# Sliding-window attention in front of a gated feed-forward: from two stages to one woven schedule

## The chip, the cores and the metric

The kernel runs on one core of a Trainium2 chip. A core has five engines, each with an instruction queue of its own that it works through in order: TensorE (PE in the profile, with its weight loads shown as PEld), VectorE (DVE), ScalarE (ACT), GpSimd (POOL) and SyncE (SP). TensorE writes its results to PSUM, a small memory of eight banks, one of which holds a 128x512 fp32 tile; the other operands live in SBUF. DMA engines move data between main memory and SBUF; POOL and SP issue the transfers here. A DMA issued by POOL can convert fp32 to bf16 on its way, and all loads of this kernel do so.

The metric is the device time of one execution in microseconds (us). Lower is better.

## The reference

For 4 batches, 8 heads, 768 tokens and 64 channels a head, each token attends to the 128 latest tokens, itself included, and to the first 4 tokens of its batch (the sinks):

```python
keep = is_sink | in_window              # pos < 4, or 0 <= i - j < 128
scores = np.where(keep, scale * (q @ k.T), -1e9)
a = softmax(scores)
attn = a @ v                            # [4, 8, 768, 64]
```

The result, written as x with 3072 rows (batch, token) and 512 columns (head, channel), goes through a feed-forward with 1536 hidden channels:

```python
g = x @ w_gate
out = ((g * sigmoid(g)) * (x @ w_val)) @ w_out      # [3072, 512] fp32
```

## The kernel before

Two stages follow each other. In the attention stage a loop runs over 16 pairs of heads (4 batches, 2 heads at a time). `load_pair` loads q, k and v of a pair with six DMAs on POOL (lines 204 to 217; the first pair's k in four smaller ones). `prep_pair` transposes q and k in blocks of 128x128 on TensorE (line 231) and copies them from PSUM to SBUF on DVE (234). Then a loop runs over the 6 tiles of 128 tokens. `attn_scores` multiplies the tile's queries with up to three blocks of 128 keys: its own, the one before and the one that holds the sinks (line 254, keys on the output's partitions, 64 rows of the PE array a head), applies exp on ACT (261) and multiplies by a mask of zeros and ones on DVE (265). `attn_pv` multiplies by v, which carries a 65th column of ones so that the sum of each softmax row comes out beside the result (275), and DVE divides by that sum (282, 283). `flush_tile` transposes the normalised tile on TensorE (291), and ACT copies it into xT (292), which holds the whole transposed x.

The feed-forward stage, `ffn_chunks`, runs over 6 blocks of 512 tokens. For each of 12 slices of 128 hidden channels four matmuls of 512 columns give the gate, `pg` (line 138), four more the value, `pv` (144); ACT computes Silu (149) and DVE the product (150). Then 4 down tiles of 128 tokens take 12 matmuls each (157), ACT copies the result (162), and POOL and SP in turn issue the store (163).

The six PSUM pools have one buffer for each of their names, and several names are used in turn by both stages. The order of the program text isn't the order of the run: the framework's scheduler orders each engine's instructions by its own priorities and buffers. So the weights' 20 DMAs (lines 119 to 124), which the text places near the end of the attention stage, are issued well before it. A slot mechanism that would have let feed-forward pieces into the attention stage (`Feed`) is switched off.

## Time and profile before

| what | value |
|---|---|
| three timed runs, median (lowest to highest) | 376.04 us (375.91 to 376.06) |
| profiled execution: first to last instruction | 374.3 us |
| PE busy in it | 346.1 us (92%) |
| DVE, ACT, POOL busy | 154.9, 150.2, 104.2 us |
| read from, written to main memory | 28.31 MB, 6.29 MB |

The profile is of one execution, which has no separate time beside its span; the median lies 1.7 us above the span. PE's matmuls are pipelined and their ends are modelled: a matmul is shown as busy from its start until its result stands in PSUM, so short matmuls that wait for one another make PE look busy too. The groups of instructions give the busy time, then the mean duration of one in nanoseconds, then how long the engine had been idle before them and what ended that. The granted clock of TensorE is 0.999 of full speed over the span.

### The profile page before, as it was taken

How to read it: one execution, taken by the hardware profiler on the slowest of the kernel's cores; microseconds unless marked ns; L12 is line 12 of the kernel's file. 1: busy time of each engine (PE TensorE's matmuls, PEld its weight loads, DVE VectorE, ACT ScalarE, POOL GpSimd, SP SyncE). 2: the span in 40 equal slices, each digit the busy share in tenths (PEclk: the TensorE clock that was granted, in tenths of full speed). 3: DMA queues.
4: the chain of work that ended last, by engine and by line, in shares of the span. 5: the costliest groups of instructions: out<-in, count | busy, mean ns of one | idle time of the engine just before them, and what ended most of it. 6: DMA issues, size and time to landing. Idle time of an engine off the chain costs nothing.

```text
span 374.3 us, 5659 instructions
## 1 busy us (share of the span) xinstructions
PE 346.1 (92%) x2112; PEld 172.9 (46%) x2112; DVE 154.9 (41%) x440; ACT 150.2 (40%) x386; POOL 104.2 (28%) x155
## 2 busy tenths in 40 slices
PE   0689999999999999899999999999999999999995
PEld 0355555555555555554444444443444444444442
DVE  0466666666666666664330232033023203302320
ACT  1355555555655655566331332333133233313321
POOL 8997666965445551110001000000100000010000
PEclk9999999999999999999999999999999999999999
DMA  9999999998998983330001100200110020011002
GB/s 60 67 98 120 147 183 174 135 130 59 60 64 59 57 59 21 23 21 2 0 0 58 56 0 12 103 0 3 56 56 2 3 109 2 0 56 58 0 10 102
DMA packets 80890, 20.80 MB, mean 56 GB/s; under 512 B 76000, under 2 KB 77536, under 8 KB 80864
## 3 DMA queue, kind: packets, MB, share of 16 engines
q0 software_dynamic: 79136, 17.31, 49.6%
q1 hardware_dynamic: 1728, 3.15, 2.2%
q8 instruction: 16, 0.26, 0.3%
q14 instruction: 10, 0.08, 0.1%
HBM read 28.31 MB, written 6.29 MB: 92 GB/s over the span
## 4 chain that ended last, share of the span: by engine, by line
PE 85%; POOL 5%; ACT 4%; DMA 2%; issue 2%; DVE 0%; POOLq 0%; ACTq 0%; DVEq 0%
PE pv L144 19%; PE pg L138 17%; PE po L157 17%; PE ps L254 15%; PE po L275 8%; PE pt L231 7%; ACT pe L261 4%; PE px L291 3%; DMA wo<-in_moe_w_out_dram 1%; POOL va L217 1%; POOL qb L215 1%; DMA kb<-in_k_dram 1%; POOL kb L204 1%; POOL kb L211 0%; DVE ht L150 0%
## 5 line engine op out<-in xcount | busy, mean ns | idle before, releaser
L150 DVE TENSOR_TENSOR ht<-sg,pv 128x512 bf16<-128x512 bf16 x72 | 49.5, 687 | 135.5 <-PE pv L144 135.5
L261 ACT ACTIVATE pe<-ps 128x384 bf16<-128x384 f32 (+1 forms) x192 | 73.3, 435 | 79.2 <-PE po L275 64.6
L254 PE MATMUL ps<-qT,kT 64*128 64x128 bf16 x480 | 76.0, 293 | 9.4 <-ACT pe L261 6.9
L149 ACT ACTIVATE sg<-pg 128x512 bf16<-128x512 f32 x72 | 43.0, 597 | 83.5 <-PE pg L138 83.5
L138 PE MATMUL pg<-xT,wg 128*128 128x512 bf16 x288 | 75.4, 383 | 0.2 <-ACT pe L261 0.2
L144 PE MATMUL pv<-xT,wv 128*128 128x512 bf16 x288 | 74.8, 381 | 0.3 <-DVE ht L150 0.3
L157 PE MATMUL po<-wo,ht 128*128 128x512 bf16 x288 | 63.1, 379 | 0.0
L163 POOL DMA_DIRECT2D out_dram<-ot x12 | 6.6, 547 | 202.3 <-ACT ot L162 202.3
L254 PEld LDWEIGHTS <-kT 64*128 64x128 bf16 x480 | 34.4, 111 | 32.4 <-issue 15.4
L144 PEld LDWEIGHTS <-wv 128*128 128x128 bf16 x288 | 27.9, 97 | 44.0 <-issue 18.2
L275 PE MATMUL po<-va,pe 128*128 128x65 bf16 x480 | 44.5, 244 | 1.6 <-DVE an L283 1.5
L157 PEld LDWEIGHTS <-ht 128*128 128x128 bf16 x288 | 28.2, 98 | 34.0
L138 PEld LDWEIGHTS <-wg 128*128 128x128 bf16 x288 | 28.2, 98 | 33.8 <-issue 0.6
L265 DVE TENSOR_TENSOR pe<-pe,mask_g 128x768 bf16<-128x768 bf16 x64 | 35.7, 557 | 18.0 <-ACT pe L261 16.3
L275 PEld LDWEIGHTS <-pe 128*128 128x128 bf16 x480 | 31.9, 128 | 15.9 <-issue 9.4
L162 ACT COPY ot<-po 128x512 f32<-128x512 f32 x24 | 14.1, 586 | 54.3 <-PE po L157 54.3
L217 POOL DMA_DIRECT2D va<-in_v_dram x32 | 26.4, 831 | 30.0 <-PE po L275 29.5
L215 POOL DMA_DIRECT2D qb<-in_q_dram x32 | 26.5, 835 | 18.7 <-PE pt L231 18.5
L231 PE MATMUL pt<-ident_b,kb 128*128 128x128 bf16 x96 | 18.0, 296 | 11.9 <-POOL ident_b masks.py:199 8.7
L211 POOL DMA_DIRECT2D kb<-in_k_dram x30 | 24.8, 838 | 13.0 <-PE po L275 11.0
L283 DVE TENSOR_TENSOR an<-po,rcp 128x128 bf16<-128x128 f32 x96 | 27.5, 286 | 1.3
L291 PE MATMUL px<-ident_b,an 128*128 128x128 bf16 x96 | 27.9, 290 | 0.1
(33 smaller groups left out, 146.6 us busy)
## 6 DMA issues: line engine op xcount, KB each, us to landing
qb<-in_q_dram POOLq DMA_DIRECT2D x32, 96.0 KB, 3.4
va<-in_v_dram POOLq DMA_DIRECT2D x32, 96.0 KB, 3.7
out_dram<-ot POOLq DMA_DIRECT2D x12, 256.0 KB, 2.3
out_dram<-ot SPq DMA_DIRECT2D x12, 256.0 KB, 2.0
kb<-in_k_dram POOLq DMA_DIRECT2D x30, 96.0 KB, 3.5
wg<-in_moe_w_gate_dram POOLq DMA_DIRECT2D x4, 384.0 KB, 6.8
wv<-in_moe_w_val_dram POOLq DMA_DIRECT2D x4, 384.0 KB, 6.5
wo<-in_moe_w_out_dram POOLq DMA_DIRECT2D x12, 128.0 KB, 4.4
```

The source lines that it names most:

```text
L138: nc.tensor.matmul(pg, wg[:, c, f * P:(f + 1) * P], xT[:, c, tb0:tb0 + TB], start=(c == 0), stop=(c == DMC - 1),)
L144: nc.tensor.matmul(pv, wv[:, c, f * P:(f + 1) * P], xT[:, c, tb0:tb0 + TB], start=(c == 0), stop=(c == DMC - 1),)
L149: nc.scalar.activation(sg, pg, AF.Silu)
L150: nc.vector.tensor_tensor(ht[:, f], sg, pv, op=ALU.mult)
L157: nc.tensor.matmul(po, ht[:, f, ts * P:(ts + 1) * P], wo[:, f], start=(f == 0), stop=(f == DFC - 1),)
L215: nc.gpsimd.dma_start(qb[:, :, hh], q[b, h + hh].rearrange(rr, p=P))
L231: nc.tensor.transpose(pt[:, j * P:(j + 1) * P], src[:, half * 3 + j], ident_b,)
L254: nc.tensor.matmul(pss[hh][:, j * P:(j + 1) * P], kT[r0:r0 + D, kv * P:(kv + 1) * P], qT[r0:r0 + D, t * P:(t + 1) * P], start=True, stop=True,
L261: nc.scalar.activation(pe[:, hh, :nb * P], pss[hh][:, :nb * P], AF.Exp, scale=scale)
L265: nc.vector.tensor_tensor(pe4, pe4, masks[t][:, :, :nb, :], op=ALU.mult,)
L275: nc.tensor.matmul(po[:, hh], pe[:, hh, j * P:(j + 1) * P], va[:, kv, hh], start=(j == 0), stop=(j == nb - 1),)
L291: nc.tensor.transpose(px, anat_tiles[t], ident_b)
```

## The change

The whole body of the kernel is replaced. The result is the same function.

- The order is fixed: under `manual_schedule` each engine gets its instructions in the order of the program text.
- Attention is cut into 12 groups of 256 tokens with all 8 heads. A group g belongs to batch b = g // 3 and stands at place c = g % 3 in it; c = 0 has no earlier keys. It consists of steps: T transposes q and k of a pair of heads (four times a group), S computes scores and exp of a pair (four times), K the sinks (once, if c > 0), PV multiplies 128 tokens and four heads by v (four times) and X transposes the result (twice). Masks, divisions and copies of X on DVE are put into a list, `later`, and issued at the end of the current piece.
- The sinks' scores for all heads come from four accumulating matmuls: `kss` holds the 4 sink keys of the 8 heads at 32 columns of their own, and `vsbs` the 4 sink values of each head in rows of their own. `step_ks` fills both, the second from `vcs`, which 8 small DMAs a batch bring.
- Groups 0 and 1 come first. In feed-forward block tb = 0 to 4 the steps of groups 2 tb + 2 and 2 tb + 3 are placed in 15 of 16 slots: a gate slot takes them between pg and pv, a down slot in the middle of its 12 matmuls.
- Silu becomes a tanh: (tanh(g/2) + 1) * g is twice Silu(g), and the final copy is scaled by 0.5. The tanh is kept in fp32.
- pg, pv and the down tiles share three PSUM buffers; scores have one (two banks), P·V results two, and one buffer serves T, K and X. xT holds two blocks.
- The loads of groups 0 to 3 and of all weights, masks and small DMAs stand in one fixed order on POOL; the load of group g + 4 follows T of group g. All stores are issued by SP.

```diff
-            nc.scalar.activation(sg, pg, AF.Silu)
-            nc.vector.tensor_tensor(ht[:, f], sg, pv, op=ALU.mult)
-            yield
...
-            nc.scalar.copy(out=ot, in_=po)
-            (nc.sync if ts % 2 else nc.gpsimd).dma_start(
...
+    natp = pool("natp", 4)
+    vpool = pool("vpool", 1)
+    kqtp = pool("kqtp", 2)
+    epool = pool("epool", 3)
+    espool = pool("espool", 2)
+    xnp = pool("xnp", 3)
+    smallp = pool("smallp", 4)
+    xtp = pool("xtp", 2)
+    tpool = pool("tpool", 3)
+    upool = pool("upool", 3)
+    hpool = pool("hpool", 2)
+    opool = pool("opool", 4)
+    ps_f = pool("ps_f", 3, True)
+    ps_s = pool("ps_s", 1, True)
+    ps_o = pool("ps_o", 2, True)
+    ps_t = pool("ps_t", 1, True)
+    ctx.enter_context(tc.manual_schedule())
...
+    def load_group(g, split=1):
+        b, c = divmod(g, GC)
+        t0 = c * 256
+        kq = natp.tile([P, 2, 2, H * D], BF16, tag="kq", name="kq")
+        va = vpool.tile([P, 2, H, VS], BF16, tag=f"va{g}", name="va")
+        hn = H // split
+        for s in range(split):
+            hs = slice(s * hn, (s + 1) * hn)
+            for i, src in ((0, k), (1, q)):
+                for j in range(2):
+                    nc.gpsimd.dma_start(
+                        kq[:, i, j, s * hn * D:(s + 1) * hn * D].rearrange(
+                            "p (h d) -> p h d", d=D),
+                        src[b, hs, t0 + j * P:t0 + (j + 1) * P].rearrange(
+                            "h p d -> p h d"),
+                    )
+        for j in range(2):
+            nc.gpsimd.dma_start(
+                va[:, j, :, 0:D],
+                v[b, :, t0 + j * P:t0 + (j + 1) * P].rearrange("h p d -> p h d"),
+            )
+        nat[g], vas[g] = kq, va
...
+    def load_gate(i):
+        n = FG * P
+        for lst, w, nm in ((wgs, moe_w_gate, "wg"), (wvs, moe_w_val, "wv")):
+            t = wpool.tile([P, DMC, n], BF16, tag=f"{nm}{i}", name=nm)
+            nc.gpsimd.dma_start(
+                t, w[:, i * n:(i + 1) * n].rearrange("(c p) f -> p c f", p=P))
+            lst.append(t)
...
+    def load_out(i):
+        n = DFC // 4
+        t = wpool.tile([P, n, DM], BF16, tag=f"wo{i}", name="wo")
+        nc.gpsimd.dma_start(
+            t, moe_w_out[i * n * P:(i + 1) * n * P].rearrange("(c p) f -> p c f", p=P))
+        wos.append(t)
...
+    load_group(0, split=2)
+    make_identity(nc, ident)
...
+    load_group(1)
+    build_mask(mask0, True)
+    load_gate(0)
+    load_gate(1)
+    build_mask(mask, False)
+    load_gate(2)
+    load_gate(3)
+    load_group(2)
+    nc.gpsimd.memset(diag_h, 1.0)
+    nc.gpsimd.affine_select(
+        out=diag_h, in_=diag_h, compare_op=ALU.is_ge, fill=0.0, base=0,
+        pattern=[[-NS, H]], channel_multiplier=1)
+    nc.gpsimd.affine_select(
+        out=diag_h, in_=diag_h, compare_op=ALU.is_ge, fill=0.0, base=NS - 1,
+        pattern=[[NS, H]], channel_multiplier=-1)
+    KS = P + 2 * NS
+    for b in range(B):
+        vc = const.tile([P, D + 1], BF16, tag=f"vc{b}", name="vc")
+        nc.vector.memset(vc, 0.0)
+        nc.vector.memset(vc[:, D:D + 1], 1.0)
+        ks = const.tile([P, NP2 * KS], BF16, tag=f"ks{b}", name="ks")
+        nc.vector.memset(ks, 0.0)
+        vsb = const.tile([P, H, D + 1], BF16, tag=f"vsb{b}", name="vsb")
+        vcs.append(vc)
+        kss.append(ks)
+        vsbs.append(vsb)
+    for i in range(4):
+        load_out(i)
+    load_group(3)
+    for b in range(B):
+        for h in range(H):
+            nc.gpsimd.dma_start(vcs[b][h * NS:(h + 1) * NS, 0:D], v[b, h, 0:NS])
+    def ones_v(g):
+        nc.vector.memset(vas[g][:, :, :, D:D + 1], 1.0)
...
+    def flush():
+        for f in later:
+            f()
+        later.clear()
+    def step_T(g, p, on_dve=False):
+        b, c = divmod(g, GC)
+        if c == 0 and p == 0:
+            kqT[b] = kqtp.tile([P, NP2, 2, S], BF16, tag="kqT", name="kqT")
+        pt = ps_t.tile([P, 2, 2, P], BF16, tag="pt", name="pt")
+        for i in range(2):
+            for t in range(2):
+                nc.tensor.transpose(
+                    pt[:, i, t], nat[g][:, i, t, p * P:(p + 1) * P], ident)
+        dst = kqT[b][:, p, :, c * 256:(c + 1) * 256].rearrange(
+            "q i (t r) -> q i t r", t=2)
+        if on_dve:
+            nc.vector.tensor_copy(out=dst, in_=pt)
+        else:
+            nc.scalar.copy(out=dst, in_=pt)
+    def step_ks(g):
+        b = g // GC
+        dst = kss[b].rearrange("q (a m) -> q a m", m=KS)
+        for h in range(2):
+            r = slice(h * D, (h + 1) * D)
+            nc.vector.tensor_copy(
+                out=dst[r, :, h * NS:(h + 1) * NS], in_=kqT[b][r, :, 0, 0:NS])
+        nc.vector.tensor_tensor(
+            vsbs[b],
+            vcs[b].rearrange("q (o d) -> q o d", o=1).broadcast_to([P, H, D + 1]),
+            diag_h.rearrange("q (h o) -> q h o", o=1).broadcast_to([P, H, D + 1]),
+            op=ALU.mult)
+    def step_S(g, p):
+        b, c = divmod(g, GC)
+        if p == 0:
+            e_t[g] = epool.tile([P, H, 512], BF16, tag="e", name="e")
+        ps = ps_s.tile([P, 2, 512], FP32, tag="s", name="s")
+        kT, qT = kqT[b][:, p, 0], kqT[b][:, p, 1]
+        q0 = c * 256
+        parts = [(q0, q0, 256, P), (q0 + P, q0 + P, P, 3 * P)]
+        if c > 0:
+            parts.insert(0, (q0 - P, q0, P, 0))
+        for kk, qq, n, col in parts:
+            for h in range(2):
+                r = slice(h * D, (h + 1) * D)
+                nc.tensor.matmul(
+                    ps[:, h, col:col + n], kT[r, kk:kk + P], qT[r, qq:qq + n],
+                    start=True, stop=True)
+        lo = 0 if c > 0 else P
+        e = e_t[g][:, 2 * p:2 * p + 2, lo:512]
+        nc.scalar.activation(e, ps[:, :, lo:512], AF.Exp, scale=scale)
+        m = (mask if c > 0 else mask0).rearrange("q (o a) x -> q o (a x)", o=1)
+        def dve():
+            nc.vector.tensor_tensor(
+                e, e, m[:, :, lo:512].broadcast_to([P, 2, 512 - lo]), op=ALU.mult)
+        later.append(dve)
+    def step_K(g):
+        b, c = divmod(g, GC)
+        if c == 0:
+            return
+        ps = ps_t.tile([P, 256], FP32, tag="pt", name="pk")
+        for p in range(NP2):
+            nc.tensor.matmul(
+                ps, kss[b][:, p * P:(p + 1) * P],
+                kqT[b][:, p, 1, c * 256:(c + 1) * 256],
+                start=(p == 0), stop=(p == NP2 - 1))
+        es_t[g] = espool.tile([P, 256], BF16, tag="es", name="es")
+        nc.scalar.activation(es_t[g], ps, AF.Exp, scale=scale)
+    def step_PV(g, j, hh):
+        b, c = divmod(g, GC)
+        t = 2 * c + j
+        if hh == 0:
+            xns[g, j] = xnp.tile([P, DM], BF16, tag="xn", name="xn")
+        po = ps_o.tile([P, 4, D + 1], FP32, tag="o", name="o")
+        mms = []
+        if c > 0:
+            mms.append((po, es_t[g][:, j * P:(j + 1) * P],
+                        vsbs[b][:, 4 * hh:4 * hh + 4]))
+        for hq in range(4):
+            h = 4 * hh + hq
+            if t > 0:
+                vp = vas[g][:, 0, h, 0:D + 1] if j else vas[g - 1][:, 1, h, 0:D + 1]
+                mms.append((po[:, hq], e_t[g][:, h, 256 * j:256 * j + P], vp))
+            mms.append((po[:, hq], e_t[g][:, h, 256 * j + P:256 * (j + 1)],
+                        vas[g][:, j, h, 0:D + 1]))
+        for i, (o, l, r) in enumerate(mms):
+            nc.tensor.matmul(o, l, r, start=(i == 0), stop=(i == len(mms) - 1),
+                             skip_group_check=True)
+        def dve():
+            rcp = smallp.tile([P, 4, 1], FP32, tag="rcp", name="rcp")
+            nc.vector.reciprocal(rcp, po[:, :, D:D + 1])
+            nc.vector.tensor_tensor(
+                xns[g, j][:, 256 * hh:256 * (hh + 1)].rearrange(
+                    "p (h d) -> p h d", h=4),
+                po[:, :, 0:D], rcp.broadcast_to([P, 4, D]), op=ALU.mult)
+        later.append(dve)
+    def step_X(g, j):
+        tb, off = divmod(g * 256 + j * P, TB)
+        if off == 0:
+            xTs[tb] = xtp.tile([P, DMC, TB], BF16, tag="xT", name="xT")
+        pt = ps_t.tile([P, DMC, P], BF16, tag="pt", name="px")
+        for i in range(DMC):
+            nc.tensor.transpose(pt[:, i], xns[g, j][:, i * P:(i + 1) * P], ident)
+        def dve():
+            nc.vector.tensor_copy(out=xTs[tb][:, :, off:off + P], in_=pt)
+        later.append(dve)
+    def T(g, p):
+        def f(pro=False):
+            if p == 0:
+                ones_v(g)
+            step_T(g, p, on_dve=(pro and p % 2 == 1))
+            if p == NP2 - 1:
+                if g % GC == 0:
+                    later.append(lambda: step_ks(g))
+                if g + 4 < NG:
+                    load_group(g + 4)
+        return f
+    def A(fn, *a):
+        def f(pro=False):
+            if pro and fn is not step_S:
+                flush()
+            fn(*a)
+        return f
...
+    def gate(tb, f, attn):
+        fi, fo = divmod(f, FG)
+        fs = slice(fo * P, (fo + 1) * P)
+        if f == 0:
+            hts[tb] = hpool.tile([P, DFC, TB], BF16, tag="ht", name="ht")
+        x = xTs[tb]
+        pg = ps_f.tile([P, TB], FP32, tag="f", name="pg")
         for c in range(DMC):
+            nc.tensor.matmul(pg, wgs[fi][:, c, fs], x[:, c],
+                             start=(c == 0), stop=(c == DMC - 1))
+        th = tpool.tile([P, TB], FP32, tag="th", name="th")
+        nc.scalar.activation(th, pg, AF.Tanh, scale=0.5)
+        for a in attn:
+            a()
+        pv = ps_f.tile([P, TB], FP32, tag="f", name="pv")
+        for c in range(DMC):
+            nc.tensor.matmul(pv, wvs[fi][:, c, fs], x[:, c],
+                             start=(c == 0), stop=(c == DMC - 1))
+        u = upool.tile([P, TB], BF16, tag="u", name="u")
+        nc.vector.scalar_tensor_tensor(u, th, 1.0, pg, op0=ALU.add, op1=ALU.mult)
+        nc.vector.tensor_tensor(hts[tb][:, f], u, pv, op=ALU.mult)
+        flush()
+    def down(tb, ts, attn):
+        po = ps_f.tile([P, DM], FP32, tag="f", name="pd")
+        n = DFC // 4
         for f in range(DFC):
+            if f == DFC // 2:
+                for a in attn:
+                    a()
+            nc.tensor.matmul(
+                po, hts[tb][:, f, ts * P:(ts + 1) * P], wos[f // n][:, f % n],
+                start=(f == 0), stop=(f == DFC - 1))
+        ot = opool.tile([P, DM], FP32, tag="ot", name="ot")
+        nc.scalar.activation(ot, po, AF.Copy, scale=0.5)
+        nc.sync.dma_start(out[tb * TB + ts * P:tb * TB + (ts + 1) * P], ot)
+        flush()
+    def run(*steps):
+        for s in steps:
+            s(pro=True)
+            if len(later) > 1:
+                later.pop(0)()
+    def ts(g):
+        return [T(g, p) for p in range(NP2)], [A(step_S, g, p) for p in range(NP2)]
+    def px(g):
+        return ([A(step_PV, g, j, hh) for j in range(2) for hh in range(2)],
+                [A(step_X, g, j) for j in range(2)])
+    t0, s0 = ts(0)
+    t1, s1 = ts(1)
+    v0, x0 = px(0)
+    v1, x1 = px(1)
+    run(*t0)
+    run(s0[0], s0[1], s0[2], t1[0], s0[3], t1[1], t1[2], t1[3])
+    run(v0[0], s1[0], v0[1], s1[1], v0[2], s1[2], v0[3], s1[3],
+        A(step_K, 1), x0[0], x0[1])
+    run(*v1, *x1)
+    flush()
+    for tb in range(NTB):
+        slots = [[] for _ in range(16)]
+        if tb + 1 < NTB:
+            ga, gb = 2 * tb + 2, 2 * tb + 3
+            ta, sa = ts(ga)
+            tb_, sb = ts(gb)
+            va_, xa = px(ga)
+            vb, xb = px(gb)
+            slots = [
+                [ta[0], ta[1]], [ta[2], ta[3]], [sa[0]], [sa[1], A(step_K, ga)],
+                [sa[2], tb_[0]], [sa[3], tb_[1]], [va_[0], tb_[2]],
+                [va_[1], tb_[3]], [va_[2], sb[0], A(step_K, gb)], [va_[3], sb[1]],
+                [xa[0], sb[2]], [xa[1], sb[3]],
+                [vb[0], vb[1]], [vb[2], vb[3], xb[0]], [xb[1]], [],
+            ]
+        for f in range(DFC):
+            gate(tb, f, slots[f])
+        for s in range(TB // P):
+            down(tb, s, slots[DFC + s])
...
```

320 lines of the change are left out of this document (44 added, 276 removed).

## The prediction

> **What bounds the kernel now.** The page first: span, the engines' slices and the chain that ended last.
>
> ```profile
> span 374.3 us, 5659 instructions
> ...
> PE   0689999999999999899999999999999999999995
> DVE  0466666666666666664330232033023203302320
> ...
> PE 85%; POOL 5%; ACT 4%; DMA 2%; issue 2%; DVE 0%; POOLq 0%; ACTq 0%; DVEq 0%
> ```
>
> The chain is PE almost throughout, but DVE shows two stages: attention up to slice 17, feed-forward after it. The busy times by stage (columns: length, then busy us and instructions of PE, PEld, DVE, ACT, POOL, then clock, DMA share, GB/s):
>
> ```profile
> 0.00:10.00 10.00, 0.86 (x6) 0.73 (x7) 0.48 (x3) 1.28 (x1) 8.87 (x20) 1.00 0.93 59
> 12.00:172.00 160.00, 145.99 (x1218) 86.38 (x1217) 102.75 (x357) 89.56 (x284) 86.72 (x122) 1.00 1.05 86
> 172.80:370.60 197.80, 197.31 (x882) 84.84 (x880) 50.72 (x78) 57.97 (x101) 6.56 (x12) 1.00 0.08 31
> ```
>
> Attention puts about 1218 small matmuls into 160 us, 0.13 us each. What they cost without waits is seen in runs of weight loads, which pace them, and the wide ones in the chain in order of time (start, length):
>
> ```profile
> 102.52 0.24 PEld L231 LDWEIGHTS <-qb 128*128 128x128 bf16 x3 [0.19 <-issue]
> 17.48 0.34 PEld L254 LDWEIGHTS <-kT 64*128 64x128 bf16 x8 [0.20 <-issue]
> 103.17 0.35 PEld L275 LDWEIGHTS <-pe 128*128 128x128 bf16 x6
> ...
> 358.27 0.86 PE pg L138 x4
> 359.14 1.01 PE pv L144 x4
> 360.14 10.37 PE po L157 x48
> ```
>
> So a transpose costs 0.08, a score 0.043, a P·V matmul 0.058 us; a 512-column matmul 10.37/48 = 0.216. Attention's PE stream is about half its 160 us; the rest is the round trip scores, exp, mask, P·V, normalise. Feed-forward is within 6% of its 864 x 0.216 = 186.6 us; the excess is pv, 1.01 where pg takes 0.86 (pv has one buffer, freed by DVE).
>
> **The change: the woven blocks.** The round trips of ten of the twelve 256-token groups move under feed-forward blocks 0 to 4, where PE has wide matmuls meanwhile. A group with predecessors (c > 0) streams 16 transposes 1.28, scores 4 x (4 x 0.043 + 2 x 0.10) = 1.49, sink scores 4 x 0.108 = 0.43, P·V 4 x (8 x 0.058 + 0.11) = 2.30, X transposes 8 x 0.08 = 0.64: 6.1 us. The 256-column score isn't in the trace: two narrow ones, 0.086, or half a wide one, 0.108; I take 0.10. A group with c = 0 has fewer scores and no sinks: 1.28 + 1.14 + 24 x 0.058 + 0.64 = 4.5. Seven of the one and three of the other: 56.3 us, 11.3 a block. With 144 x 0.216 = 31.1 a block streams for 42.4 us. Three buffers shared by pg, pv and down remove the 0.15 wait before pv.
>
> Do ACT and DVE keep up? The groups by line (mean ns after the busy time):
>
> ```profile
> L149 ACT ACTIVATE sg<-pg 128x512 bf16<-128x512 f32 x72 | 43.0, 597 | 83.5 <-PE pg L138 83.5
> L261 ACT ACTIVATE pe<-ps 128x384 bf16<-128x384 f32 x128 | 55.8, 488 | 39.0 <-PE po L275 34.5 <-PE ps L254 4.3
> L261 ACT ACTIVATE pe<-ps 128x256 bf16<-128x256 f32 x32 | 10.5, 382 | 16.3 <-PE po L275 16.3
> L162 ACT COPY ot<-po 128x512 f32<-128x512 f32 x24 | 14.1, 586 | 54.3 <-PE po L157 54.3
> L150 DVE TENSOR_TENSOR ht<-sg,pv 128x512 bf16<-128x512 bf16 x72 | 49.5, 687 | 135.5 <-PE pv L144 135.5
> L265 DVE TENSOR_TENSOR pe<-pe,mask_g 128x768 bf16<-128x768 bf16 x64 | 35.7, 557 | 18.0 <-ACT pe L261 16.3
> L283 DVE TENSOR_TENSOR an<-po,rcp 128x128 bf16<-128x128 f32 x96 | 27.5, 286 | 1.3
> L282 DVE RECIPROCAL rcp<-po 128x2 f32<-128x2 f32 x96 | 16.4, 170 | 23.6 <-PE po L275 22.1
> L234 DVE COPY kT<-pt 128x384 bf16<-128x384 bf16 x32 | 11.2, 350 | 13.2 <-PE pt L231 12.5 <-PE ps L254 0.2
> ```
>
> ACT grows 0.106 us per 128 columns, so the 1024-column exp is 0.488 + 5 x 0.106 = 1.02; tanh as Silu, 0.60; the 512-column copy of a transpose 0.59. A block: 12 x 0.60 + 8 x 0.59 + 8 x 1.02 + 2 x 0.38 + 4 x 0.59 = 23 us. DVE: the new (tanh + 1) x pg has fp32 inputs, not in the trace; nearest is L150, 0.69 (the low end), twice that the high end; I take 0.69, as L150 reads PSUM too. The 1024-column mask product is 0.70 by L265's slope, 1.37 by L150's rate; 0.70, the same operands. Normalising 256 columns 0.17 + 0.43, copying X 0.46. A block: 12 x 1.38 + 8 x 0.70 + 8 x 0.60 + 4 x 0.46 = 29 us. Both lie under PE's 42 and cost nothing while they stay in their gate; each gate's attention sits between pg and pv on PE's fixed order, so where they don't, pv and all behind it wait. Three places: gates 0 and 1 put two transpose steps on one ps_t buffer; the second waits for tanh and the first's copy, 0.2 + 0.60 + 0.59 after pg, less its own 0.3, thus 1.2 each, 2.5 with the wake-up; gate 11's X transpose waits for gate 10's copy on DVE behind a product (0.5); the second P·V of the first down tile waits for the last mask (0.7). Together 3.7. Bounds: 0, and 9 a block (15 insertions at 0.6, one round trip). A block is 46.1; five 230.5. At the high DVE prices gates with both a mask and a normalise need 2.06 + 1.37 + 0.6 = 4.0 on DVE against 2.7 on PE, inside the upper bound. Block 5 has no attention: 31.1 + 0.5. From its last matmul, 360.14 + 10.37, to the end stay 3.8 us. The 24 stores all go to SP, one per down tile of 12 x 0.216 = 2.6 us; one lands in 2.0 (last row of the next fence).
>
> **The change: the start.** Weights, issued under attention from 33 to 78 us so far, now stand in POOL's queue ahead of the first block. The issue costs, the first and last weight issue, and what the queue moved:
>
> ```profile
> L204 POOL DMA_DIRECT2D kb<-in_k_dram x4 | 3.2, 801 | 0.8 <-POOLq L367 0.8
> L211 POOL DMA_DIRECT2D kb<-in_k_dram x30 | 24.8, 838 | 13.0 <-PE po L275 11.0 <-PE px L291 1.9
> L119 POOL DMA_DIRECT2D wg<-in_moe_w_gate_dram x4 | 2.3, 575 | 0.0
> L163 POOL DMA_DIRECT2D out_dram<-ot x12 | 6.6, 547 | 202.3 <-ACT ot L162 202.3
> 14.43 0.59 POOL L81 MEMSET mask_t<- 128x512 bf16 x1
> 33.02 0.57 POOL L119 DMA_DIRECT2D wg<-in_moe_w_gate_dram  x1
> 76.93 1.12 POOL L124 DMA_DIRECT2D wo<-in_moe_w_out_dram  x2
> L107 POOL TENSOR_SCALAR_AFFINE_SELECT mask_g<-mask_g 128x128 bf16<-128x128 bf16 x2 | 0.6, 284 | 0.0
> ...
> DMA packets 8755, 1.12 MB, mean 112 GB/s; under 512 B 8753, under 2 KB 8753, under 8 KB 8753
> DMA packets 5190, 1.80 MB, mean 180 GB/s; under 512 B 4803, under 2 KB 4803, under 8 KB 5189
> kb<-in_k_dram POOLq DMA_DIRECT2D x4, 48.0 KB, 2.5
> out_dram<-ot SPq DMA_DIRECT2D x12, 256.0 KB, 2.0
> ```
>
> The two packet rows are 20 to 30 us (q, k, v alone) and 50 to 60 us (with weights). What matters is one wait. step_ks(0) multiplies vcs[0], whose eight small DMAs POOL issues last, after groups 0 to 3 and all weights. That product enters DVE's queue behind the first transposes; queued behind it are group 0's masks and the copy of T(1,1), and behind that copy (one ps_t buffer) PE's T(1,2) and everything after. So attention stops until vcs[0] lands.
>
> When? POOL: 1.3; group 0 8 x 0.80 + 2 x 0.86 (1024 runs, by the slope from 384 to 768), identity 0.6, group 1 6 x 0.86: 15.3; first mask 0.59 + 7 x 0.28: 17.8; four gate loads 3.2 (512 runs: 0.58 to 0.84, I take 0.80), second mask 1.7, four more 3.2, group 2 5.2, small selects 0.7, four down loads 2.8, group 3 5.2, eight small DMAs at 0.55: 44.2; landing 2.5: 46.7. The DMA engines: 3.15 MB of groups and 4.72 MB of weights, of which 1.57 by 17.8 us; the other 6.3 at 180 GB/s end at 53, with groups at 112 at 58. Bounds 46 and 58; I take 52.
>
> Then DVE clears vsbs and three masks (0.45 + 3 x 0.56), T(1,1) to T(1,3) take 2 more: PE goes on at +4.5. Group 1's four scores share one ps_s buffer: matmuls, exp and two hand-overs, 1.7 each, 6.8. Sinks, four P·V at 0.7, normalise and two X transposes with copies: 5.5. Block 0 starts 17 us after (13 to 20), at 69 (59 to 78).
>
> PE idles from about 25 to 52 us; the row 0 to 10 us has 8.7 of idling and still clock 1.00, so I charge nothing. The Trainium skill (TensorE: Matmul & The Clock Gate, Part 1: The HAM clock gate) says that a PE left idle drops to half its clock and needs about 3.4 us of activity to get it back. By that rule the sum would be higher by an estimated 2 us (half of 3.4); the row above doesn't agree.
>
> **Sum.** 69 + 230.5 + 31.6 + 3.8 = 334.9 us against the span of 374.3. The timed median, 376.04, lies 1.7 above that span: 337.
>
> **Rivals.** *The start isn't held:* vcs[0] lands early or that product delays nothing. Then transposes of group 2 (slot 0) wait for its load at about 41 us and those of group 3 (slot 4) for 53, so block 0 starts in effect at 45, 24 earlier: 313. For it, landings of a few us; against it, one queue in order. *Every weave stalls:* 15 insertions at 0.6 make 9 a block instead of 3.7, 27 in all: 364. For it, attention now loses half its PE time to such hand-overs; against it, most steps' inputs are a gate old. *Table switching, the slower side:* were tanh and exp in different tables, each of 40 woven exps would pay two loads:
>
> ```profile
> L261 ACT ACT_TABLE_LOAD x1 | 1.3, 1283 | 0.8 <-PEq L367 0.8
> L149 ACT ACT_TABLE_LOAD x1 | 1.3, 1283 | 0.0
> ```
>
> ACT then needs 0.60 + 1.28 + 1.02 + 1.28 = 4.2 in a gate of 2.4: 1.8 x 40 = 72 more, 409. It decides from 39/40 = 1.0 us per exp. For it: exp and Silu each loaded one; no row shows tanh. The Trainium skill (ScalarE: Activation LUTs, Table sets: the hidden batching unit) puts exp and tanh in one set; by that there is one load in all, and nothing changes in the sum.
>
> **How the numbers follow.** Forecast 0.61 (by itself 322 to 352: start 62 to 76, stalls 2.5 to 6 a block), unheld start 0.17, stalls everywhere 0.18, tables 0.04. The range 305 to 364 takes in the first rival with a faster stream and most of the second; outside lie the tables and about half of the second's upper tail. Within 0.2% of before, what a measurement of this kernel can tell from no change, would take two errors that cancel: 0.01. Slower: 0.05, the tables and what none of this foresees. Faster 0.94.
>
> **What would show it.** DVE's waits should have vsbs waiting for the vcs DMA, some 35 us, ending at 46 to 58 us; if not, the first rival. First pg at 59 to 78 us. Windows over blocks 0 to 4: 46 us each, PE waiting in gates 0 and 1 for ACT's copy of the transposes. One table load. Block 5 at 31 to 32 us, no gap before pv. The forecast is wrong if block 0 starts before 55, if a woven block takes over 50, or if DVE's fp32 product takes over 1 us.

## The result, and the profile after

The changed kernel takes 328.47 us (median of four runs, 327.02 to 330.5) where the kernel before takes 376.05 beside it on the same chip: a ratio of 0.8738, 95% interval 0.8701 to 0.8776, so 12.6% less. The forecast was 337 (305 to 364). The profiled execution has a span of 325.2 us; the median lies 3.3 above it (before: 1.7). These four runs lie 3.5 us apart, so kernels that differ by less are compared here by the stages of their traces.

The page after: span, two engines' busy tenths in 40 slices, and the chain that ended last, by engine.

```profile
span 325.2 us, 4622 instructions
...
PE   0420000576999988999979999799997999999995
...
DVE  2200000663788526886158882378842688617830
...
PE 63%; DVE 13%; DMA 9%; POOL 7%; ACT 5%; issue 2%; DVEq 0%; POOLq 0%
```

Two things differ from before. PE does nothing in slices 3 to 6 (24 to 57 us), and from slice 9 on DVE is busy beside it, where before it went down to 2 and 3 tenths. The chain has a new stretch of DMA and POOL: the start. The stages, in the view by windows (length, then busy us and instructions of PE, PEld, DVE, ACT, POOL, then clock, DMA share, GB/s):

```profile
19.00:56.00 37.00, 0.21 (x3) 0.05 (x1) 0.00 (x0) 0.51 (x1) 25.47 (x42) 1.00 1.50 170
56.00:74.40 18.40, 11.14 (x113) 8.00 (x112) 12.27 (x33) 5.01 (x6) 18.40 (x31) 1.00 0.67 43
74.40:117.40 43.00, 40.27 (x297) 20.24 (x297) 27.20 (x58) 20.26 (x32) 13.43 (x16) 1.00 0.93 75
117.40:161.10 43.70, 41.39 (x321) 21.40 (x320) 26.93 (x54) 22.03 (x34) 10.51 (x12) 1.00 0.63 62
...
246.60:290.40 43.80, 41.49 (x322) 21.45 (x321) 26.85 (x53) 22.04 (x34) 0.00 (x0) 1.00 0.07 25
290.40:325.20 34.80, 31.22 (x145) 13.99 (x143) 16.51 (x24) 10.15 (x17) 0.00 (x0) 1.00 0.10 38
```

The first row is the hole: 37 us in which PE, DVE and ACT together work for under 1 us while POOL issues loads. The five woven blocks take 43.0, 43.7, 42.5, 43.0 and 43.8, 216.0 in all; the last block 31.2 and the tail 3.6. So 74.4 + 216.0 + 31.2 + 3.6 = 325.2.

What ends the hole, and what the first woven gate looks like, stands in the timeline (start, length, engine, line; in brackets how long the engine had been idle and what released it):

```profile
56.14 0.70 DVE L223 TENSOR_TENSOR vsb<-vc,diag_h 128x520 bf16<-128x520 bf16 x1 [40.58 <-DMA vc<-in_v_dram]
...
58.17 0.42 DVE L211 COPY kqT<-pt 128x512 bf16<-128x512 bf16 x1
58.65 0.58 PE L206 MATMUL pt<-ident,kq 128*128 128x128 bf16 x4 [39.43 <-DVE kqT L211]
...
74.40 1.02 PE L340 MATMUL pg<-xT,wg 128*128 128x512 bf16 x4 [0.52 <-DVE xT L307]
75.26 0.39 PE L206 MATMUL pt<-ident,kq 128*128 128x128 bf16 x4
76.58 0.38 PE L206 MATMUL pt<-ident,kq 128*128 128x128 bf16 x4 [0.94 <-ACT kqT L213]
76.80 1.03 PE L348 MATMUL pv<-xT,wv 128*128 128x512 bf16 x4
...
81.90 0.40 PE L242 MATMUL s<-kqT 64*128 64x128 bf16 x6
82.22 1.04 PE L348 MATMUL pv<-xT,wv 128*128 128x512 bf16 x4
...
91.33 0.27 PE L286 MATMUL o<-vsb,es 128*128 128x260 bf16 x1
91.44 0.41 PE L286 MATMUL o<-va,e 128*128 128x65 bf16 x8
91.68 0.39 PE L206 MATMUL pt<-ident,kq 128*128 128x128 bf16 x4
91.90 1.03 PE L348 MATMUL pv<-xT,wv 128*128 128x512 bf16 x4
```

The product of vsbs waited 40.58 us for the small DMAs of vcs[0]; three masks and one copy behind it on DVE, PE resumed after 39.43 us without work. That is the chain of waits that the prediction named. In gate 0 the second transpose step starts 1.32 us after the first, which itself takes 0.22: the stall on the one ps_t buffer. The starts also give the price of a step: six score matmuls 0.32, nine P·V matmuls 0.35, four transposes 0.22.

### The profile page after: what moved, and what is told of

It reads as the page before. It is cut to its first block, busy times and chain, and to the rows that moved or that the text cites. A ratio compares the mean times of both kernels' runs of the same rounds, so it can differ in the third digit from the quotient of the medians.

```text
span 325.2 us, 4622 instructions
## 1 busy us (share of the span) xinstructions
PE 251.2 (77%) x1824; PEld 128.8 (40%) x1824; DVE 167.9 (52%) x352; ACT 127.2 (39%) x197; POOL 95.8 (29%) x142
## 4 chain that ended last, share of the span: by engine, by line
PE 63%; DVE 13%; DMA 9%; POOL 7%; ACT 5%; issue 2%; DVEq 0%; POOLq 0%
PE pd L363 18%; PE pv L348 16%; PE pg L340 15%; DVE ht L353 4%; PE o L286 4%; PE s L242 3%; PE pt L206 3%; DMA wg<-in_moe_w_gate_dram 3%; DMA va<-in_v_dram 3%; POOL kq L89 3%; DMA wo<-in_moe_w_out_dram 3%; DVE e L251 2%; DVE u L352 2%; ACT th L343 2%; PE px L304 2%
## 5 line engine op out<-in xcount | busy, mean ns | idle before, releaser
L352 DVE SCALAR_TENSOR_TENSOR u<-th,pg 128x512 bf16<-128x512 f32 x72 | 49.4, 686 | 40.8 <-ACT th L343 39.9
L343 ACT ACTIVATE th<-pg 128x512 f32<-128x512 f32 x72 | 43.0, 597 | 69.4 <-PE pg L340 69.4
L206 PE MATMUL pt<-ident,kq 128*128 128x128 bf16 x192 | 20.2, 233 | 61.2 <-DVE kqT L211 39.9
L363 PE MATMUL pd<-wo,ht 128*128 128x512 bf16 x288 | 65.6, 379 | 0.0
L353 DVE TENSOR_TENSOR ht<-u,pv 128x512 bf16<-128x512 bf16 x72 | 49.5, 688 | 24.1 <-PE pv L348 19.5
L247 ACT ACTIVATE e<-s 128x1024 bf16<-128x1024 f32 (+1 forms) x48 | 45.6, 950 | 9.9 <-PE s L242 9.3
L213 ACT COPY kqT<-pt 128x512 bf16<-128x512 bf16 x44 | 25.8, 585 | 54.6 <-PE pt L206 54.6
L89 POOL DMA_DIRECT2D kq<-in_k_dram x26 | 22.6, 882 | 77.7 <-PE pt L206 76.7
L251 DVE TENSOR_TENSOR e<-e,mask 128x1024 bf16<-128x1024 bf16 (+1 forms) x48 | 30.6, 640 | 1.8 <-ACT e L247 1.8
L89 POOL DMA_DIRECT2D kq<-in_q_dram x26 | 22.6, 885 | 0.8 <-DMA wv<-in_moe_w_val_dram 0.8
L292 DVE TENSOR_TENSOR xn<-o,rcp 128x256 bf16<-128x256 f32 x48 | 20.4, 425 | 1.7
```

The costliest lines, as they stand in the source:

```text
L89: nc.gpsimd.dma_start(kq[:, i, j, s * hn * D:(s + 1) * hn * D].rearrange("p (h d) -> p h d", d=D), src[b, hs, t0 + j * P:t0 + (j + 1) * P] ...
L206: nc.tensor.transpose(pt[:, i, t], nat[g][:, i, t, p * P:(p + 1) * P], ident)
L247: nc.scalar.activation(e, ps[:, :, lo:512], AF.Exp, scale=scale)
L251: nc.vector.tensor_tensor(e, e, m[:, :, lo:512].broadcast_to([P, 2, 512 - lo]), op=ALU.mult)
L343: nc.scalar.activation(th, pg, AF.Tanh, scale=0.5)
L352: nc.vector.scalar_tensor_tensor(u, th, 1.0, pg, op0=ALU.add, op1=ALU.mult)
```

## The experiments

The theory: the start is held by data that nobody needs early (vcs[0]) and costs some 30 us; in the blocks attention costs its PE stream plus three small stalls. Rivals: attention's stalls everywhere, the tables, and, after the first look, the clock of PE.

**Issue vcs[0] right behind group 0 (e1_vc_early).** Its eight small DMAs move there, and the clearing of its tile ahead of them.

```diff
+    KS = P + 2 * NS
+    for b in range(B):
+        vc = const.tile([P, D + 1], BF16, tag=f"vc{b}", name="vc")
...
     load_group(0, split=2)
+    for h in range(H):
+        nc.gpsimd.dma_start(vcs[0][h * NS:(h + 1) * NS, 0:D], v[0, h, 0:NS])
...
-    for b in range(B):
+    for b in range(1, B):
```

> Only the place of eight small DMAs changes: vcs[0] is loaded right behind group 0 instead of last. Theory (the start is held by DVE's product with vcs[0], released at 56.1 us, block 0 at 74.4): the wait of vsb for vc falls from 40.6 to under 10 us; the prologue then runs as fast as its own steps, block 0 could begin near 40, but group 2 (for slot 0) stands behind all gate weights and lands at about 43, group 3 (for slot 4) at 54 to 57; so some 26 to 30 us are saved: ratio to the changed kernel about 0.91, 298 to 303 us. Rival (the weights and groups themselves set the start, DVE's wait only shows it): under 8 us saved, 320 us or more.

309.6 us (309.5 to 312.71), ratio 0.8259 (0.822 to 0.8298): the wait is worth 19 us at once, but 7 us less than expected. The timeline shows why:

```profile
36.87 0.87 POOL L96 DMA_DIRECT2D va<-in_v_dram  x1 [1.06 <-DMA wv<-in_moe_w_val_dram]
37.73 0.12 POOL L175 MEMSET diag_h<- 128x8 bf16 x1
...
38.41 0.70 DVE L225 TENSOR_TENSOR vsb<-vc,diag_h 128x520 bf16<-128x520 bf16 x1 [18.84 <-POOL diag_h L179]
```

The same product has a second late operand: diag_h, which POOL builds behind group 2's loads. Neither the prediction nor this expectation had it. And POOL itself is late, since it waits 1.06 us for a gate load before it issues va.

**One DMA for the eight (e6_one_vc).** Here vcs keeps its place in the queue.

```diff
-        for h in range(H):
-            nc.gpsimd.dma_start(vcs[b][h * NS:(h + 1) * NS, 0:D], v[b, h, 0:NS])
+        nc.gpsimd.dma_start(vcs[b][0:H * NS, 0:D], v[b, :, 0:NS])
```

> The 32 small DMAs become 4, one for each batch, at the same place in POOL's order. If the bytes in front of vcs[0] set its landing (group 3's v landed at 53.6), the end of DVE's wait moves from 56.1 to 53 to 55 and the time by 1 to 3 us, 325 to 327. If POOL's eight issues with a wait each set it (47.6 to 54.3 us, 0.4 to 1.3 of waiting before each), vcs[0] lands about 50 and the time falls by 5 to 7, 321 to 323.

325.38 us (325.34 to 326.55), ratio 0.8666 (0.865 to 0.8682). The product still waits until 54.77 instead of 56.14, and block 0 starts 1.2 us earlier. The one DMA is issued at 48.10 and takes over 6 us to arrive, where the last of the eight, issued at 53.83, took 1.6: mostly the bytes in front, not the number of issues, set when vcs[0] lands.

**T's copies alternate between DVE and ACT (e2_t_dve).** The first copy of each pair of transposes in gates 0 and 1 no longer waits for tanh.

```diff
-            step_T(g, p, on_dve=(pro and p % 2 == 1))
+            step_T(g, p, on_dve=(p % 2 == 1 if pro else p % 2 == 0))
```

> In the woven blocks the copy of the first transpose step of each pair goes to DVE instead of ACT, so that it does not stand behind the tanh. Theory (gates 0 and 1 wait 1.1 us each for tanh and copy): the second step then waits about 0.5, so 0.6 x 2 x 5 = 6 us less, 321 to 324. Rival (DVE has no room or the wait moves to the next step): within 2 us of the changed kernel.

323.01 us (322.83 to 326.02), ratio 0.8614 (0.8576 to 0.8652). Gates 0 and 1 take 2.85 instead of 3.27 us: 0.42 x 10 = 4.2 us, somewhat under the 6 expected, as 0.52 us of the wait stay. The 5.5 us between the medians is a little more than that; the spans differ by 4.0.

**Attention between the blocks instead of inside them (e3_lump).** Gates and down tiles get no steps; after each block the next two groups run in the order of the first two.

```diff
-            gate(tb, f, slots[f])
+            gate(tb, f, [])
...
-            down(tb, s, slots[DFC + s])
+            down(tb, s, [])
+        if tb + 1 < NTB:
+            run(*ta)
...
+            run(*vb, *xb)
+            flush()
```

> The same steps and order within attention, but all steps of the two groups stand between two feed-forward blocks instead of inside them. Theory (weaving hides the round trips): a block without attention takes 31.1 to 31.6 as block 5 does, and two groups in one piece 22 to 26 us, as the prologue does from its first transposes to block 0 without its wait; so 54 to 58 a block instead of 43.2, 55 to 75 us more in all, 383 to 403 us, no faster than the kernel before. Rival (the new steps are cheap by themselves, the gain is in the tiling): under 25 us more, below 355. In the lumps PE should show the long matmuls of the prologue (256 columns: about 0.41 us instead of 0.27), if its clock follows its load.

402.01 us (401.32 to 402.7), ratio 1.0693 (1.0671 to 1.0715), at the upper end of what was expected: slower than the kernel before. The weave is worth 402.01 - 328.47 = 73.5 us, more than the whole gain; without it the rest of the change taken together loses. A lump and the feed-forward block after it, by windows:

```profile
106.00:129.80 23.80, 15.16 (x149) 10.26 (x148) 13.19 (x36) 10.19 (x14) 10.51 (x12) 0.59 1.07 78
130.00:162.00 32.00, 32.00 (x140) 14.06 (x139) 16.58 (x25) 8.96 (x15) 0.00 (x0) 0.94 0.05 18
```

The lumps of two groups take 24 to 27 us where the same steps add 12 to a woven block, and the granted clock of this one is 0.59. It goes down inside the lump: six score matmuls take 0.39 us at 109.20 and 0.61 at 110.71, and PE's waits in the lump up to there are 0.52 to 1.12 us each. So a chain of small matmuls with such waits is enough to lose the clock.

**Silu again (e4_silu).**

```diff
-        th = tpool.tile([P, TB], FP32, tag="th", name="th")
-        nc.scalar.activation(th, pg, AF.Tanh, scale=0.5)
+        th = tpool.tile([P, TB], BF16, tag="th", name="th")
+        nc.scalar.activation(th, pg, AF.Silu)
...
-        nc.vector.scalar_tensor_tensor(u, th, 1.0, pg, op0=ALU.add, op1=ALU.mult)
-        nc.vector.tensor_tensor(hts[tb][:, f], u, pv, op=ALU.mult)
+        nc.vector.tensor_tensor(hts[tb][:, f], th, pv, op=ALU.mult)
...
-        nc.scalar.activation(ot, po, AF.Copy, scale=0.5)
+        nc.scalar.activation(ot, po, AF.Copy)
```

> The gate is again Silu on ACT and one product on DVE; all else as in the changed kernel. If tanh is there to keep one activation table: each of 40 woven exps brings two loads of 1.28 us, ACT needs 4.2 us in a gate of 2.4, so 60 to 80 us more, 385 to 405 us, with 80 or more table loads. Rival (the loads hide under PE or Silu is in the table of exp): two loads, and within 5 us of the changed kernel, or less by the shorter DVE work.

403.21 us (401.02 to 405.4), ratio 1.0725 (1.0665 to 1.0785). The groups by line (instructions, then busy us and mean ns):

```profile
L343 ACT ACT_TABLE_LOAD x41 | 52.6, 1283 | 0.7
L247 ACT ACT_TABLE_LOAD x40 | 51.3, 1283 | 0.7
```

81 loads of 1.28 us, two per woven exp, and 74.7 us more than with tanh, although DVE has one product less in each gate. The Trainium skill (ScalarE: Activation LUTs, Table sets: the hidden batching unit) puts exp and tanh into one set; the trace agrees: the changed kernel has one load in all.

**Keep PE busy through the hole (e5_warm).** 168 matmuls on the identity, result unused, stand where PE would wait.

```diff
-    run(s0[0], s0[1], s0[2], t1[0], s0[3], t1[1], t1[2], t1[3])
+    def warm(pro=False):
+        pw = ps_f.tile([P, TB], FP32, tag="f", name="pw")
+        for _ in range(168):
+            nc.tensor.matmul(pw, ident, mask0.rearrange("p a x -> p (a x)"),
+                             start=True, stop=True)
+    run(s0[0], s0[1], s0[2], t1[0], s0[3], t1[1], warm, t1[2], t1[3])
```

> 168 matmuls of 512 columns that compute nothing are put where PE waits for the vcs (18.6 to 58.6 us); nothing else changes. If PE runs at half its clock after the wait because it idled, the first matmuls after it get as short as in the blocks (four transposes 0.39 instead of 0.58 us), and block 0 begins 0.5 to 2 us earlier; if it runs slow there because the chain of steps itself is sparse, they are short for the first few us only and long again later, and the gain is under 1 us. If the clock is not the cause, all stay as long as they were.

327.81 us (327.49 to 330.93), ratio 0.8738 (0.8702 to 0.8774): nothing gained. By windows, and in the timeline of DVE and PE:

```profile
25.00:56.00 31.00, 31.00 (x145) 14.07 (x144) 0.00 (x0) 0.00 (x0) 18.52 (x29) 1.00 1.57 173
56.00:66.00 10.00, 4.93 (x51) 3.15 (x50) 5.95 (x16) 2.88 (x4) 10.00 (x21) 0.63 0.05 3
66.00:75.60 9.60, 6.84 (x67) 5.10 (x65) 6.30 (x18) 2.13 (x3) 9.60 (x13) 0.50 1.26 80
75.60:86.00 10.40, 8.71 (x42) 3.91 (x41) 2.79 (x5) 3.40 (x7) 4.30 (x6) 0.67 1.23 80
...
57.16 0.70 DVE L223 TENSOR_TENSOR vsb<-vc,diag_h 128x520 bf16<-128x520 bf16 x1 [41.59 <-DMA vc<-in_v_dram]
...
59.66 0.58 PE L206 MATMUL pt<-ident,kq 128*128 128x128 bf16 x4 [3.24 <-DVE kqT L211]
```

The dummies run at full speed (31.00 us for 145) but end at 56.4, before the product of vsbs, and PE then waits 3.24 us. The first four transposes behind that wait already take 0.58 us, as in the changed kernel, and the clock goes down about there: it is 1.00 from 56 to 58 us and 0.64 from 58 to 60. So none of the expectation's branches was tried as it was meant, since the dummies did not reach to the release. What the trace does show is that the slow clock, once there, stays through group 1, whose chain of hand-overs keeps PE busy for 49% and 71% of the two windows, and into block 0 (gates 0 and 1 take 5.11 and 4.12 us instead of 3.27).

**No sinks (e7_no_sink).** K, its exp, the ninth P·V matmul, vsbs and the small DMAs are left out for the groups with c > 0.

```diff
...
-        b, c = divmod(g, GC)
-        if c == 0:
-            return
+        return
...
-        if c > 0:
+        if False:
...
-                    later.append(lambda: step_ks(g))
+                    pass
```

> Left out: the sinks of all groups with c > 0 (the sink scores, their exp, their share of P.V, the filling of kss and vsbs, and the small DMAs); so it computes less than the reference. Against the early vcs alone it has the same start, and shows what the sinks cost in the blocks: 8 groups x (0.45 + 4 x 0.11) = 7 us of PE's stream by the changed kernel's trace. So 291 to 297 if the early vcs alone gives 300; the start is not held. If the start is held by the bytes instead, 314 to 321.

288.22 us (287.7 to 290.88), ratio 0.768 (0.7649 to 0.7712), a little less than expected. Block 0 starts at 34.53, and then gate 0 takes 9.54 us, as its first transpose waits 2.60 us for group 2's k and three more for theirs: the next late data. The later blocks are 0.7 to 1.4 us shorter, the sinks' own cost. By the spans, 38.7 us apart, the start gives 39.9, the four later blocks 4.7, and block 0 takes 5.9 back.

**Groups 2 and 3 ahead of most weights, on top of e1 (e8_order).**

```diff
     load_gate(0)
+    load_group(2)
     load_gate(1)
     build_mask(mask, False)
+    load_group(3)
     load_gate(2)
     load_gate(3)
-    load_group(2)
...
-    load_group(3)
```

> vcs[0] early as in the first of these runs, and the loads in the order of need: group 1, gate weights 0, group 2, gate weights 1, group 3, gate weights 2 and 3, down weights. Theory: what held the start after the early vcs was the order of the bytes; group 2 now lands near 27 and group 3 near 36, block 0 begins at 36 to 40 and does not stall; 8 to 12 us less than with the early vcs alone, 288 to 293 us. Rival (the total of bytes sets it): no gain over the early vcs alone.

315.66 us (314.7 to 315.8), ratio 0.8401 (0.8387 to 0.8415): a miss by some 23 us, and slower than e1. The product of vsbs now runs at 41.20, after 21.65 us of waiting for diag_h, which stands behind still more loads. So diag_h, not only vcs, holds the start. The product is 2.8 us later than in e1 and block 0 starts 3.1 later (59.66 instead of 56.55); another 2.1 us are lost in block 0, whose first gates run slowly (5.11 and 3.72 us instead of 3.27).

**Both operands early (e9_vc_diag).** e1 with diag_h built right after the identity.

```diff
     make_identity(nc, ident)
+    nc.gpsimd.memset(diag_h, 1.0)
+    nc.gpsimd.affine_select(
...
-    nc.gpsimd.memset(diag_h, 1.0)
-    nc.gpsimd.affine_select(
...
```

> As the early vcs, and diag_h, the other operand of DVE's product, is built on POOL right behind the identity instead of behind group 2's loads. Theory (in the early-vcs run the same product held DVE 18.8 us more, for diag_h, and block 0 began at 56.6): now DVE is free by 15 us, the prologue ends near 40; group 2 lands at about 44, so gate 0 waits some 4 to 6 us and PE starts at half clock; 8 to 11 us less than 309.6: 298 to 302 us. Rival (the prologue's own chain or the loads hold it): within 3 us of 309.6.

300.21 us (298.9 to 301.27), ratio 0.7985 (0.7952 to 0.8017): as expected. The product runs at 19.02 without a wait. The timeline of PE at block 0:

```profile
40.09 1.02 PE L342 MATMUL pg<-xT,wg 128*128 128x512 bf16 x4 [0.52 <-DVE xT L309]
42.92 0.29 PE L208 MATMUL pt<-ident,kq 128*128 128x128 bf16 x1 [1.81 <-DMA kq<-in_k_dram]
...
45.73 0.29 PE L208 MATMUL pt<-ident,kq 128*128 128x128 bf16 x1 [0.58 <-DMA kq<-in_q_dram]
...
47.07 1.91 PE L350 MATMUL pv<-xT,wv 128*128 128x512 bf16 x4
```

Group 2's loads arrive at 42.9 to 45.7. During that wait PE does four small matmuls, and the four of pv behind it take 1.91 us where those of pg took 1.02, and the clock recorded there is 0.50.

**e9 with groups 2 and 3 ahead (e10_order_diag).** The moves of e8 and e9 together.

```diff
     make_identity(nc, ident)
+    nc.gpsimd.memset(diag_h, 1.0)
...
     load_gate(0)
+    load_group(2)
     load_gate(1)
     build_mask(mask, False)
+    load_group(3)
```

> The run before this one, with the loads in the order of need (group 2 behind the first gate weights, group 3 behind the second). Theory (the order-of-need run was slower than the early vcs alone only because its longer queue put diag_h at 41 instead of 38 us): block 0 begins near 40 without a wait for group 2, 290 to 296 us, 5 to 9 less than with the loads in the old order. Rival (order of need is worse by itself, for instance by gate weights that come late): 300 us or more, with PE waiting for wg or wv.

297.3 us (295.84 to 298.84), ratio 0.7923 (0.7881 to 0.7964), about 1 us above what was expected, and 2.9 under e9 where 5 to 9 were expected. Block 0 starts later (42.75 instead of 40.09) but no gate waits for group 2 any more (gate 0 takes 3.27 instead of 8.69).

**One T a gate (e11_spread).** The order before the blocks is that of the changed kernel; only the slots differ.

```diff
-                [ta[0], ta[1]], [ta[2], ta[3]], [sa[0]], [sa[1], A(step_K, ga)],
-                [sa[2], tb_[0]], [sa[3], tb_[1]], [va_[0], tb_[2]],
-                [va_[1], tb_[3]], [va_[2], sb[0], A(step_K, gb)], [va_[3], sb[1]],
+                [ta[0]], [ta[1]], [ta[2], sa[0]], [ta[3], sa[1]],
+                [sa[2], A(step_K, ga)], [sa[3], tb_[0]], [va_[0], tb_[1]],
+                [va_[1], tb_[2]], [va_[2], tb_[3], sb[0]],
+                [va_[3], sb[1], A(step_K, gb)], [xa[0], sb[2]], [xa[1], sb[3]],
```

> The changed kernel with another placing of the steps: one transpose step a gate (gates 0 to 3 and 5 to 8) instead of two in gates 0 and 1; the start stays as it is. Theory (each of the two gates loses 1.1 us in waiting for the one ps_t buffer): gates 0 to 3 take about 1.95, 1.95, 2.4 and 2.4 us instead of 3.27, 3.27, 2.16 and 2.59, and a block 2 to 2.5 us less; 317 to 320 us. Rival (the wait moves to later gates): 325 or more.

319.06 us (317.27 to 319.5), ratio 0.8479 (0.8454 to 0.8504): as expected. From block 1 on gates 0 and 1 take 1.95 instead of 3.27 and a block 40.2 to 41.5, 1.7 to 2.3 less. In this trace block 0 gains nothing: its gate 0 still runs slowly (3.79) and gate 11 waits 1.60 for a copy of X. The pair's stall was the largest in a block, and where nothing shares the buffer within a gate it is gone.

**All of it (e12_all).** The order of e10, with the identity ahead of group 0 and diag_h behind group 1; one DMA per batch for vcs, as in e6; the slots of e11.

```diff
+    make_identity(nc, ident)
     load_group(0, split=2)
+    nc.gpsimd.dma_start(vcs[0][0:H * NS, 0:D], v[0, :, 0:NS])
...
     load_group(1)
+    nc.gpsimd.memset(diag_h, 1.0)
...
     load_gate(0)
+    load_group(2)
     load_gate(1)
     build_mask(mask, False)
+    load_group(3)
...
```

> All together: identity first, one small DMA for each batch's sink values and that of batch 0 behind group 0, diag_h behind group 1, the loads in the order of need, and one transpose step a gate. If the parts add up: the start of block 0 at 35 to 38 us instead of 74.4, and 2 to 2.5 us less a block; 276 to 284 us. If the loads bound the start in their sum, 285 to 295.

283.12 us (281.43 to 283.8), ratio 0.7525 (0.75 to 0.7551), in the range that was expected: a quarter less than before and 45 us less than the changed kernel. Its span is 281.5: block 0 starts at 39.21 instead of 74.40 (35.2 earlier, but after the 35 to 38 that were expected), the five blocks take 207.4 instead of 216.0 (8.6 less). The product's wait is down to 3.12 us, but a third late operand comes up behind it: DVE waits 4.74 us for the second mask, which POOL builds behind group 2's loads, and PE waits 3.31 us with it. pg of gate 0 runs at the slow rate:

```profile
15.92 0.70 DVE L222 TENSOR_TENSOR vsb<-vc,diag_h 128x520 bf16<-128x520 bf16 x1 [3.12 <-POOL diag_h L169]
...
28.59 0.69 DVE L250 TENSOR_TENSOR e<-e,mask 128x1024 bf16<-128x1024 bf16 x1 [4.74 <-POOL mask L155]
...
39.21 1.87 PE L339 MATMUL pg<-xT,wg 128*128 128x512 bf16 x4 [0.52 <-DVE xT L306]
...
42.68 1.03 PE L339 MATMUL pg<-xT,wg 128*128 128x512 bf16 x4
```

## Why the prediction was right, and which steps were off

**The start: mechanism right, 5.4 us too early.** Block 0 was forecast at 69 and came at 74.40. The landing of vcs[0], taken at 52 (46 to 58), let the product run at 56.14; the chain behind it, taken at 17, took 18.3. The prediction chose 52 between POOL's issue count (46.7) and the bytes (53 to 58), and the bytes decide. They moved at 170 GB/s in the hole, not 180; by that rate the prediction's 6.3 MB behind 17.8 us end at 55. POOL's issue count (44.2 us without a wait) is not what holds, as POOL stopped for loads in flight, about 1 us at a time.

```profile
28.74 0.88 POOL L89 DMA_DIRECT2D kq<-in_q_dram  x1 [0.85 <-DMA wv<-in_moe_w_val_dram]
30.66 0.88 POOL L96 DMA_DIRECT2D va<-in_v_dram  x1 [1.04 <-DMA wg<-in_moe_w_gate_dram]
32.56 0.88 POOL L96 DMA_DIRECT2D va<-in_v_dram  x1 [1.02 <-DMA wv<-in_moe_w_val_dram]
```

So the queue follows the landings, and the small DMAs at its end can't start before most of the bytes have arrived; e6 shows the same from the other side. That the product holds the start is shown by e9: with both operands early, block 0 starts 34.3 us earlier, and the next thing to wait for is group 2's loads. What the prediction missed is that diag_h would have held it too. It cost nothing in its sum, but e1 and e8 came out above their expectations for it.

**The woven blocks: the term that was mis-sized is attention's stream.** A block was forecast at 46.1 = 31.1 wide matmuls + 11.3 attention + 3.7 stalls; measured 216.0 / 5 = 43.2. The wide matmuls are right (the last block, with no attention, takes 31.2). By the starts in the timeline, a group with predecessors costs 4 x 0.22 + 4 x 0.32 + 0.44 + 4 x 0.35 + 2 x 0.23 = 4.5 us where 6.1 were taken, one without 3.5 where 4.5 were: (7 x 4.5 + 3 x 3.5) / 5 = 8.4 a block. The rest, 43.2 - 31.1 - 8.4 = 3.7, is the sum forecast for the stalls, though not in the same places: gates 0 and 1 lose 1.1 each (1.2 forecast) and gate 11 waits 0.43 to 0.75 for a copy of X (0.5), but the 0.7 of the first down tile does not show, and some 0.9 is spread over the gates (a step S starts 0.96 us after pg, whose matmuls take 0.86). So the step that failed is "a transpose costs 0.08, a score 0.043, a P·V matmul 0.058 us". P·V is the largest part: 2.30 a group was taken, 1.40 measured. These rates were read in before's attention stage, where PE ran at half clock. The same shapes, by line and form (mean ns is the second number), before in 12 to 172 us:

```profile
L254 PE MATMUL ps<-qT,kT 64*128 64x128 bf16 x480 | 76.0, 293 | 9.4 <-ACT pe L261 6.9
L275 PE MATMUL po<-va,pe 128*128 128x65 bf16 x462 | 43.0, 244 | 1.6 <-DVE an L283 1.5
...
L138 PE MATMUL pg<-xT,wg 128*128 128x512 bf16 x4 | 2.1, 620 | 0.2 <-ACT pe L261 0.2
```

The end of it stands in before's timeline, where one matmul of the same line takes 0.62 us, and 0.38 one microsecond later:

```profile
174.90 0.62 PE L138 MATMUL pg<-xT,wg 128*128 128x512 bf16 x1
...
175.97 0.38 PE L138 MATMUL pg<-xT,wg 128*128 128x512 bf16 x1
```

After, first at the start (56 to 74.3 us):

```profile
L286 PE MATMUL o<-va,e 128*128 128x65 bf16 x56 | 4.8, 246 | 0.0
L242 PE MATMUL s<-kqT 64*128 64x128 bf16 x16 | 2.4, 293 | 1.7 <-ACT e L247 1.7
...
L242 PE MATMUL s<-kqT 64*128 64x256 bf16 x8 | 1.8, 417 | 0.0
```

and then in the blocks (117.5 to 290 us):

```profile
L348 PE MATMUL pv<-xT,wv 128*128 128x512 bf16 x192 | 49.5, 380 | 0.0
...
L286 PE MATMUL o<-va,e 128*128 128x65 bf16 x240 | 12.1, 193 | 0.1
L242 PE MATMUL s<-kqT 64*128 64x128 bf16 x112 | 11.2, 221 | 0.0
L242 PE MATMUL s<-kqT 64*128 64x256 bf16 x64 | 8.8, 272 | 0.0
```

Before's attention and the start of after have the same long durations (293, 244 to 246), the blocks the short ones; the four 512-column matmuls that before ran inside attention took 620 ns each, against 380 in a block. That the long ones are half clock is shown by e5, the run whose trace records 0.50: from 66 to 75.6 us the same three shapes take 247, 291 and 416 ns. A duration runs until the result stands in PSUM, so it doesn't double; the starts nearly do. Eight P·V matmuls take 0.46 us at the start (69.55 to 70.01), the 0.058 each that was taken, and 0.24 in a block. The error was 11.3 - 8.4 = 2.9 a block, 14.5 in all, against 5.4 the other way at the start: that 337 was only 8.5 too high is in part luck, as two errors of opposite sign met.

**The clock sentence was wrong.** The prediction argued from a clock of 1.00 in the row 0 to 10 us that an idle PE keeps its speed. The column can't bear that, and nor can the 0.999 given for the whole of before: in after it reads 1.00 everywhere, also at the start where the same matmul takes 417 instead of 272 ns. The rule of the Trainium skill (TensorE: Matmul & The Clock Gate, Part 1: The HAM clock gate), half clock for a PE left idle and about 3.4 us of activity to return, fits e5, where the first matmuls behind 3.24 us without work are slow, and e12, where the wide matmuls from 39.21 on are slow and those from 42.68 fast, 3.5 us later. In e9, where gate 1 still waits 0.73 us for the shared buffer, the return took longer: from 47.07 to 55.69. And e3 lost the clock with waits of at most 1.12 us. The estimate of 2 us by that rule can't be checked as a sum, since the slow rates last through most of the start's 18 us and were already in the prices taken from before.

**The rivals.** An unheld start (313) did not happen; its picture of what comes next was about right: in e9 gate 0 waits for group 2's loads until 45.7, where it said 41. Stalls in every weave (364) are refuted by the 3.7 a block. Table switching was priced at 72 us by loads of 1.28; e4 made it happen and lost 74.7. **The prices** of DVE and ACT held: the fp32 product (L352) 686 ns for 0.69, the wide mask 684 for 0.70, the wide exp 1021 for 1.02, the copy of T 585 for 0.59, X 419 for 0.46. Of the prediction's own tests, block 0 came after 55, no block took over 50, and the product stayed under 1 us. The three buffers shared by pg, pv and down removed the gap before pv: the last block, 31.2, has none.

## What to carry to other kernels

In an engine that works in order, list for the first instruction that waits every operand and where in its queue each is made: one product put in line early, for data needed late, held PE for 39 us, and freeing one operand only uncovered the next (vcs, then diag_h, then the second mask). Weaving small dependent matmuls between wide ones hides their round trips and, as the same shapes show, also ran them at the full clock here, so their price is to be read from a stage where PE is dense. A step put in two places that share one buffer within a gate (two T) costs a hand-over each time; spreading them gave 7.9 us in the five blocks.

## What the runs showed of the hardware that was not expected

The granted clock shown for a slice is no evidence by itself: in after and before it reads 1.00 beside matmuls that take 417 and 620 ns, where the same shapes take 272 and 380 in the blocks. The mean duration of one shape, compared between stages, tells the clock. Sparse work is enough to lose it, without any long idle stretch: in e3 it went down in a lump in which PE's waits up to there were at most 1.12 us, and the lump's mean is 0.59. Once lost it stays lost under such work: 0.50 from 66 to 75.6 us in e5, with PE shown busy for 71%.

POOL's issue of a DMA waited, wherever it waited for a DMA in the start of the changed kernel, for the one issued eight before it (at 28.74 the second wv load, at 30.66 the third wg, at 32.56 the third wv). That at most eight are in flight from POOL is inferred from this; no run changed that number, and whether the chip or the framework sets it is not shown. The small DMAs of 0.5 KB took 0.50 us of POOL each and landed in 1.6 us (median of 32).
